# First batched stage of a four-layer kernel: normalising steps spread over evictions, transposes moved into the first block, zero matmuls while rows load

## The chip, the cores and the metric

The kernel runs on one core of a Trainium2 chip. Its engines run side by side, each with its own queue of instructions: TensorE (PE for matmuls, PEld for their weight loads), VectorE (DVE), ScalarE (ACT), GpSimd (POOL) and SyncE (SP), which only issues transfers. ACT and POOL issue transfers too, between their other instructions. The metric is the device time of one execution in microseconds (us); the time before is the median of five runs.

## The reference

Four layers, A B A B, each added to its input x of 2048 rows by 640. What matters here is layer A, whose first call is where the change lies:

```python
def _layernorm(x, axis=-1, eps=1e-05):
    m = jnp.mean(x, axis=axis, keepdims=True)
    v = jnp.var(x, axis=axis, keepdims=True)
    return (x - m) / jnp.sqrt(v + eps)
...
        for s in range(n_seg):
            xs = x[:, s * seg_len:(s + 1) * seg_len, :].copy()
            h = jnp.concatenate([mem, xs], axis=1)
            q = jnp.einsum('btd,dhe->bhte', h, Wq)
            k = jnp.einsum('btd,dhe->bhte', h, Wk)
            v = jnp.einsum('btd,dhe->bhte', h, Wv)
            ...
            o = jnp.einsum('bhte,hed->btd', o, Wo)
            mem = o[:, :M, :].copy()
            outs.append(o[:, M:, :])
...
    x = x + _A_ref(_layernorm(x, axis=-1), A_mem0, A_Wq, A_Wk, A_Wv, A_Wo, A_seg_len)
    x = x + _B_ref(_layernorm(x, axis=-1), B_wqkv, B_w_phi, B_wo)
```

There are 64 segments of 32 rows and a memory of 8 rows that passes from one segment to the next; 32 heads of 192 features. Layer B is an attention without a chain and is not touched.

## The kernel before

Layer A has two parts. `A_chain` walks through the 64 segments one after the other, since the memory of one is the output of the last. To shorten that chain, `A_pre`, the batched stage, computes ahead of it what does not depend on the memory: the last 8 rows of every segment ("tails") are projected to q, k and v for all segments at once and stored in HBM (`kqb_d`, `vb_d`). It also normalises all rows of x for the chain in the first layer (`xn_dram`), since no layer B before it has done so. The change is in this first call of `A_pre`, where `x_raw` is given.

The stage has eight blocks. A block is a half h of the segments (32 segments, 256 tail rows) and a round r of eight heads; the order is r=3 for h=0 and h=1, then r=2, r=1, r=0 (`steps`, L769). I number them 1 to 8. A block has

- K and Q: for each, six groups, each ten matmuls of 128x256 (L803) into one PSUM bank, then one eviction of 128x512 (L807);
- one store of the block's k and q to `kqb_d`, issued by ACT (L809, 1536 KB in pieces of 384 bytes);
- V: two row tiles k of four groups, each five matmuls of 128x384 (L820), an eviction (L822), and after each row tile four stores to `vb_d`, issued by POOL (L824).

There are eight PSUM banks, taken in turn, and 20 evictions in a block, by VectorE and ScalarE alternately (`Ev`, L77).

The weights of a round are 15 pieces of 384 KB, five each of Wk, Wq and Wv, issued by SP (`load_matrix`, L621) in the order of use. SP has nothing else in its queue, so it runs ahead of TensorE as far as its waits let it. Three pieces of each matrix go to slots that the next round of that kind reuses, so some pieces of r=0 wait for matmuls of r=3.

`norm_tasks` splits the normalising of one tile of 128 rows in four steps: a, the load; b, the statistics on VectorE and two casts on POOL (`ln_moments`, L216); c, two activations on ScalarE (`ln_deviation`); d, reciprocal, subtraction and scaling on VectorE (`ln_apply`) and what follows, a store to `xn_dram` or the use in the stage. `in_turn` lists these steps for many tiles so that the load of a tile stands ahead of the last three steps of the tile before it. The list `tasks` is worked off one step after each eviction (`evict`, L742): first the two tail tiles of h=1 (8 steps), then the 16 tiles of all rows (64 steps), from the first eviction of block 1. The two tail tiles of h=0 are done before block 1, in step (L762). Two buffers serve each tile kind.

`transpose_rows` (L705) turns a normalised tail tile into columns: five transposes on TensorE and one copy by VectorE or ScalarE. It is done at the start of block 1 for h=0 and at the start of block 2 for h=1 (L783).

`lay_out_wo` (L645) copies two rounds of Wo from HBM to HBM in another layout (`wo_rows`, 1920 KB each); ACT issues the two copies at the start of block 5. `build_A_consts` builds small constants at block 3. `early_wo` loads seven pieces of Wo on SP in block 8.

`A_chain` then starts with the Q projection of the first segment (L901), and `fill(FILL[li])` puts 122 weight loads of one column between it and the K projection in layer 0 (L987, L1052).

The stage's instructions stand in the order in which the program gives them on each engine (`manual_schedule`). Each transfer of SP and ACT is given one of eight completion semaphores, in turn over both engines, and waits for the transfer that had that semaphore before.

Of the kernel before, what the change touches and what calls it, by code (L numbers as in the profile page):

```python
# [8 lines left out]
P = 128  # L9
BF16 = mybir.dt.bfloat16  # L10
F32 = mybir.dt.float32
# [6 lines left out]
SLOTS = {"Q": 3, "K": 3, "V": 3}  # L18
LN_EPS = 1e-5

FILL = {0: 122, 2: 78}
SEG_FILL = 1

LATE = 64512
# [91 lines left out]
class Kernel:  # L116
# [96 lines left out]
        m = self.ln_moments(lp, xt)  # L213
        self.ln_apply(lp, xt, m, self.ln_deviation(lp, m), xn, centre, scale)

    def ln_moments(self, lp, xt):  # L216
        nc, Dm = self.nc, self.Dm
        half = Dm // 2
        stats = lp.tile([P, 2, 6], F32, name="ln_stats")
        for j in range(2):  # L220
            nc.vector.bn_stats(out=stats[:, j, :], in_=xt[:, j * half:(j + 1) * half])
        mv = lp.tile([P, 2], F32, name="ln_mv")
        nc.vector.bn_aggr(out=mv[:], in_=stats[:])
        mv16 = lp.tile([P, 2], BF16, name="ln_mv16")
        nc.gpsimd.tensor_copy(out=mv16[:], in_=mv[:])
        mvr = lp.tile([P, 2], F32, name="ln_mvr")
        nc.gpsimd.tensor_copy(out=mvr[:], in_=mv16[:])
        return mvr

    def ln_deviation(self, lp, mvr):  # L230
# [350 lines left out]
    def layer_A(self, xn_dram, at_dram, li, x_raw=None):  # L581
# [63 lines left out]
        def lay_out_wo():  # L645
            if li == 0:
                self.wo_rows = dram.tile([2, P, 7680], BF16, name="wo_rows")
                for i, r in enumerate((0, 3)):
                    nc.scalar.dma_start(out=self.wo_rows[i].rearrange("p (c m) -> p c m", m=640),
                                        in_=wov[:, 12 * r:12 * r + 12, :])  # L650

        def early_wo():
# [15 lines left out]
    def A_pre(self, xn_dram, li, load_matrix, piece, wo_mid, wo_end, lay_out_wo, early_wo, x_raw):  # L668
# [9 lines left out]
        NT = T // P  # L678
        sts = [wo_mid[:, 6144 * i:6144 * i + 192 * SH].rearrange("p (s f) -> p s f", f=192) for i in range(2)]
        vts = [wo_end[:, 1792 * i:1792 * i + 1792].rearrange("p (g f) -> p g f", f=448) for i in range(2)]  # L680
        with ExitStack() as es:
# [14 lines left out]
            def gather(dst, src, h, k, queues=None):  # L696
                xv = src.rearrange("(s t) d -> t s d", t=32)
                for t2 in range(TP):
                    e = queues[t2 % 2] if queues else nc.gpsimd if k % 2 else nc.scalar
                    e.dma_start(out=dst[SH * t2:SH * t2 + SH, :], in_=xv[24 + TP * k + t2, SH * h:SH * h + SH])  # L700
# [4 lines left out]
            def transpose_rows(xb, h, k):  # L705
                pt = ps_.tile([P, 1024], BF16, name="pt", tag="bank")
                for b in range(KC):
                    self.transp(out=pt[:, P * b:P * b + P], in_=xb.rearrange("p (q b) -> p b q", b=KC)[:, b, :],
                                identity=self.ident[:, :])
                ev.copy(out=columns(h)[:, :, P * k:P * k + P], in_=pt[:, 0:640].rearrange("p (b q) -> p b q", b=KC))  # L710

            def norm_tasks(load, done, tag="ln_xn"):

                v = {}

                def a():
                    v["x"] = lp.tile([P, self.Dm], BF16, name="ln_x")
                    load(v["x"])

                def b():  # L720
                    v["m"] = self.ln_moments(lp, v["x"])

                def c():
                    v["d"] = self.ln_deviation(lp, v["m"])

                def d():
                    xn = lp.tile([P, self.Dm], BF16, name=tag, tag=tag)
                    self.ln_apply(lp, v["x"], v["m"], v["d"], xn[:])
                    done(xn)

                return [a, b, c, d]

            def in_turn(lists):

                out = [lists[0][0]]
                for i, t in enumerate(lists):
                    if i + 1 < len(lists):
                        out.append(lists[i + 1][0])
                    out += t[1:]
                return out  # L740

            def evict(out, in_):  # L742
                ev.copy(out=out, in_=in_)
                if tasks:
                    tasks.pop(0)()

            normed = {}

            def tails(h):
                return in_turn([norm_tasks(lambda x, k=k: gather(x, x_raw, h, k),  # L750
                                           lambda xn, k=k: normed.__setitem__((h, k), xn), "ln_xt") for k in range(NT)])

            def all_rows():
                rows = [slice(P * b, P * b + P) for b in range(self.NB)]
                return in_turn([norm_tasks(lambda x, q=q: nc.gpsimd.dma_start(out=x[:], in_=x_raw[q, :]),
                                           lambda xn, q=q: nc.gpsimd.dma_start(out=xn_dram[q, :], in_=xn[:]))
                                for q in rows])

            for vt in vts:
                nc.vector.memset(vt, 0.0)  # L760
            if x_raw is not None:
                first = [norm_tasks(lambda x, k=k: gather(x, x_raw, 0, k, (nc.sync, nc.scalar)),  # L762
                                    lambda xn, k=k: normed.__setitem__((0, k), xn)) for k in range(NT)]
                for step in zip(*first):
                    for f in step:
                        f()
            turn = nv = 0
            if x_raw is not None:
                steps = [(h, ri, NR - 1 - ri) for ri in range(NR) for h in range(NH)]  # L769
# [1 line left out]
                steps = [(h, ri, ri if h == 0 and NH > 1 else NR - 1 - ri) for h in range(NH) for ri in range(NR)]  # L771
            seen = set()
            for h, ri, r in steps:
                if h not in seen:
                    seen.add(h)
                    xBT = columns(h)
                    for k in range(NT):
                        if x_raw is not None:
                            xb = normed[h, k]
                        else:  # L780
                            xb = xB[h][k % 2]
                            gather(xb, xn_dram, h, k)
                        transpose_rows(xb, h, k)  # L783
                xBT = columns(h)
                if (h, ri) == ((NH - 1, 0) if x_raw is None else (0, 2)):
                    lay_out_wo()
                st = sts[turn % 2]
                turn += 1
# [2 lines left out]
                if x_raw is not None and (h, ri) == (0, 0):  # L791
                    for h1 in range(1, NH):
                        tasks += tails(h1)
                    tasks += all_rows()
                for mi, m in enumerate("KQ"):
                    load_matrix(m, r)
# [17 lines left out]
                for k in range(NT):  # L814
                    vt = vts[nv % 2]
                    nv += 1
                    for g in range(4):
                        ps = ps_.tile([P, 512], F32, name="ps_pre", tag="bank")
                        for b in range(KC):
                            nc.tensor.matmul(ps[:, 0:384], lhsT=xBT[:, b, P * k:P * k + P],  # L820
                                             rhs=w[b][:, 384 * g:384 * g + 384], start=(b == 0), stop=(b == KC - 1))
                        evict(out=self.two_heads(vt[:, g, :]), in_=ps[:, 0:384].rearrange("p (e f) -> p e f", e=2))  # L822
                    for t2 in range(TP):
                        nc.gpsimd.dma_start(out=self.vb_d[SH * h:SH * h + SH, r, :, TP * k + t2, :],  # L824
                                            in_=vt[SH * t2:SH * t2 + SH, :, :].rearrange("p (g x) f -> p g (x f)", x=2))
# [367 lines left out]
```

## Time and profile before

| | us |
|---|---|
| median of five runs | 3762.22 |
| lowest and highest of the five | 3751.65, 3768.33 |
| the profiled execution, its own time | 3751.06 |
| span of the profiled execution | 3749.3 |
| first batched stage, from its first projection to the chain's first | 10.6 to 198.9 |

The profile page gives the span and the busy time of each engine. The other views are answers of the same trace: busy time by stretch; instructions in order of time, with the idle time of the engine before each and what ended it in square brackets; waits by line; and transfers with their median time from issue to landing. Line numbers are those of the kernel before. In the stage, transfers look like this over the first 200 us (queue 1 is SP's, queue 10 ACT's, queue 0 POOL's; then packets, MB and the share of 16 engines' time):

```profile
q1 hardware_dynamic: 10608, 26.06, 35.0%
q10 hardware_dynamic: 36183, 16.77, 30.4%
q0 software_dynamic: 4608, 12.11, 18.6%
```

### The profile page before, as it was taken

To read this page: it belongs to the slowest core of one execution; us is meant where nothing else is said; L and a number is where in the kernel's file an instruction comes from. 1 tells how busy PE (TensorE), PEld (TensorE's weight loads), DVE (VectorE), ACT (ScalarE), POOL (GpSimd) and SP (SyncE) were. 2 spreads that over 40 slices of the span, in tenths; PEclk is the share of its full clock that TensorE was granted. 3 is DMA by queue.
4 is the path that set the end of the run, shared out by engine and by line. 5 is a ranking of instruction groups with operands and counts; after the bars stand their busy time and mean duration, and the time that the engine had idled before them with its cause. 6 is when DMAs were issued, how large, how long until landed. Compare 5 with 4: busy or idle time off the path is not lost.

```text
span 3749.3 us, 169123 instructions
## 1 busy us (share of the span) xinstructions
PE 3539.8 (94%) x71064; PEld 2314.8 (62%) x71408; DVE 2364.7 (63%) x6290; ACT 2072.2 (55%) x5285; POOL 1658.2 (44%) x4363
## 2 busy tenths in 40 slices
PE   7989999999999999989899899999999999999898
PEld 5766666666666666655367566666666666665453
DVE  4456666666666666546633566666666666665565
ACT  2246666666666656546432556666666666665453
POOL 3345555555555545430342455555545555553300
PEclk9999999999999999999899999999999999999999
DMA  9788888788887878930377878878888888888200
GB/s 344 221 271 292 282 283 295 272 293 280 292 287 273 291 277 280 311 113 1 135 254 199 300 263 290 288 273 289 283 285 293 279 295 277 287 285 301 80 1 29
DMA packets 531381, 931.72 MB, mean 249 GB/s; under 512 B 141034, under 2 KB 298362, under 8 KB 530618
## 3 DMA queue, kind: packets, MB, share of 16 engines
q1 hardware_dynamic: 392794, 802.36, 60.3%
q0 software_dynamic: 68160, 88.78, 7.9%
q10 hardware_dynamic: 69664, 29.76, 3.0%
q8 instruction: 558, 9.14, 1.0%
q14 instruction: 205, 1.68, 0.1%
HBM read 852.43 MB, written 72.09 MB: 247 GB/s over the span
## 4 chain that ended last, share of the span: by engine, by line
PE 60%; DMA 10%; DVE 9%; issue 7%; ACT 6%; PEld 4%; POOL 3%; SPq 1%; POOLq 0%; ACTq 0%; DVEq 0%
PE ps_qk L901 19%; PE ps_w L977 8%; PE ps_v L901 8%; PE ps_o L951 5%; PE ps_s L943 4%; DMA arena<-wo_rows 4%; PEld L803 3%; DVE hT L857 3%; PE ps_s L1009 3%; PE ps_s L938 2%; PE ps_idle L984 2%; PE ps_qk L388 2%; ACT raw L911 2%; PE ps_pre L803 1%; DVE E L1016 1%
## 5 line engine op out<-in xcount | busy, mean ns | idle before, releaser
L901 PE MATMUL ps_qk<-arena,hT 128*32 128x384 bf16 x20480 | 1000.2, 328 | 23.7 <-DMA arena<-in_A_Wk_dram 8.9
L901 PEld LDWEIGHTS <-hT 128*32 128x32 bf16 x30720 | 737.8, 96 | 440.8 <-DVE hT L1119 29.4
L911 ACT ACTIVATE raw<-ps_qk 128x384 bf16<-128x384 f32 x1024 | 502.0, 490 | 395.0 <-PE ps_s L1009 247.6
L977 PE MATMUL ps_w<-arena,OT 128*32 128x160 bf16 x24576 | 538.5, 234 | 27.2 <-issue 18.6
L884 POOL DMA_DIRECT2D Vp<-vb x512 | 258.8, 505 | 674.9 <-PE ps_o L951 464.1
L901 PE MATMUL ps_v<-arena,hT 128*32 128x384 bf16 x10240 | 535.6, 329 | 0.0
L977 PEld LDWEIGHTS <-OT 128*32 128x32 bf16 x24576 | 433.9, 97 | 118.5 <-issue 41.3
L916 DVE STREAM_TRANSPOSE KT<-raw 128x384 bf16<-128x384 bf16 x512 | 296.1, 578 | 203.0 <-ACT raw L911 199.0
L919 DVE STREAM_TRANSPOSE QT<-raw 128x256 bf16<-128x256 bf16 x512 | 227.9, 445 | 238.6 <-ACT raw L911 197.2
L872 POOL DMA_DIRECT2D kqb<-kqb x512 | 286.0, 559 | 162.8 <-POOL KT L880 148.1
L932 DVE CAST Vp<-ps_v 64x384 bf16<-64x384 f32 x512 | 286.4, 559 | 89.9 <-ACT Vp L930 76.7
L970 POOL DMA_DIRECT2D otb<-otb x512 | 282.8, 552 | 111.3 <-DVE otb L966 91.5
L930 ACT ACTIVATE Vp<-ps_v 64x384 bf16<-64x384 f32 x512 | 246.1, 481 | 145.6 <-PE ps_v L901 109.7
L957 DVE CAST OT<-ps_o 128x192 bf16<-128x192 f32 x512 | 183.1, 358 | 221.0 <-PE ps_o L951 203.4
L1016 DVE TENSOR_TENSOR E<-E,ps_s 80x320 bf16<-80x320 bf16 x512 | 247.5, 483 | 73.2 <-ACT ps_s L1015 69.1
L995 ACT ACTIVATE E<-ps_s 80x320 bf16<-80x320 f32 x512 | 221.4, 432 | 127.4 <-PE ps_s L943 100.2
L951 PEld LDWEIGHTS <-Vp 80*128 80x128 bf16 x4096 | 183.1, 99 | 160.3 <-issue 126.1
L951 PE MATMUL ps_o<-E,Vp 80*128 80x80 bf16 x4096 | 234.2, 202 | 24.6 <-ACT Vp L930 4.5
L943 PE MATMUL ps_s<-QT,KT 128*80 128x80 bf16 (+1 forms) x3072 | 234.2, 214 | 21.2 <-DVE KT L916 10.9
L865 ACT ACTIVATE Vp<-ps_w 32x160 bf16<-32x160 f32 x512 | 150.3, 294 | 177.9 <-DVE wt L1118 149.6
L956 ACT ACTIVATE OT<-ps_o 128x192 bf16<-128x192 f32 x512 | 167.8, 328 | 143.5 <-PE ps_o L951 143.4
L943 PEld LDWEIGHTS <-KT 128*80 128x80 bf16 x3072 | 195.8, 119 | 69.8 <-issue 58.8
(148 smaller groups left out, 5456.1 us busy)
## 6 DMA issues: line engine op xcount, KB each, us to landing
arena<-wo_rows SPq DMA_DIRECT2D x792, 320.0 KB, 6.7
arena<-in_A_Wq_dram SPq DMA_DIRECT2D x427, 384.0 KB, 4.5
arena<-in_A_Wv_dram SPq DMA_DIRECT2D x427, 384.0 KB, 6.4
arena<-in_A_Wk_dram SPq DMA_DIRECT2D x768, 192.0 KB, 4.6
kqb<-arena ACTq DMA_DIRECT2D x16, 1536.0 KB, 12.0
kqb<-kqb POOLq DMA_DIRECT2D x512, 48.0 KB, 5.0
arena<-in_A_Wk_dram SPq DMA_DIRECT2D x43, 384.0 KB, 6.6
vb<-arena POOLq DMA_DIRECT2D x128, 112.0 KB, 5.4
```

The lines of the kernel that those rows point to most:

```text
L872: nc.gpsimd.dma_start(out=kqb[:], in_=self.kqb_d[s, :, r, :])
L884: nc.gpsimd.dma_start(out=Vs[n % 2][64:80, :], in_=self.vb_d[s, r].rearrange("g t f -> (g t) f"))
L901: nc.tensor.matmul(o[32 * g:32 * g + 32, 0:384], lhsT=hT[:, b, :], rhs=rhs, start=(i == 0), stop=(i == KC - 1), tile_position=(0, 32 * g), ...
L911: nc.scalar.activation(out=raw[:], in_=ps[:, 0:384], func=ACT.Copy)
L916: nc.vector.transpose(out=KT[:, :, 0:64], in_=raw[:, :].rearrange("p (c j) -> p c j", j=64))
L930: nc.scalar.activation(out=o, in_=i, func=ACT.Copy)
L932: nc.vector.tensor_copy(out=o, in_=i)
L943: nc.tensor.matmul(S[0:80, c0:c0 + 80 * (q1 - q0)], lhsT=KT[:, 3 * x + i, :], rhs=QT[:, x, q0:q1, :], start=False, stop=(x == 1 and i == 2 ...
L951: nc.tensor.matmul(O[x][:, 80 * i:80 * i + 80], lhsT=Vs[n % 2][0:80, 448 * x + k:448 * x + k + 128], rhs=E[0:80, 160 * x + 80 * e:160 * x ...
L970: nc.gpsimd.dma_start(out=self.otb_d[s, :, 96 * r:96 * r + 96], in_=otb[:, :, :].rearrange("p c t -> p (c t)"))
L977: nc.tensor.matmul(W[32 * g:32 * g + 32, 0:160], lhsT=OT[:, c, q:q + 32], rhs=w[:, 640 * i + 160 * g:640 * i + 160 * g + 160], start=(firs ...
L1016: nc.vector.tensor_tensor(out=E[0:80, 0:320], in0=E[0:80, 0:320], in1=rc, op=ALU.mult)
```

## The change

Seven things change, all but one of them in `A_pre` with `x_raw` given, that is in layer 0's stage.

1. `ln_moments` can take the engine of its two casts; the stage's tasks give VectorE instead of POOL. Layer B's calls keep POOL.
2. The list of tasks may hold empty steps, and an eviction that meets one does nothing more. The tails of h=1 get three empty steps after their two loads; the tiles of all rows get one after every two steps, so a tile takes six evictions instead of four.
3. The 16 tiles of all rows are queued from block 2 instead of block 1.
4. The transposes of h=1 are done inside block 1, after the first row tile of V.
5. `lay_out_wo` is called at the start of block 6 instead of block 5 and issued by SP instead of ACT, in the first layer.
6. Matmuls of the identity with a buffer of zeros, 128x512, into a bank of their own: 12 before the first transposes and 3 after each of the two sets of transposes of h=0. Nothing reads their result.
7. `FILL` for layer 0 goes from 122 to 86.

```diff
-FILL = {0: 122, 2: 78}
+FILL = {0: 86, 2: 78}
...
-    def ln_moments(self, lp, xt):
+    def ln_moments(self, lp, xt, cast=None):
...
-        nc.gpsimd.tensor_copy(out=mv16[:], in_=mv[:])
+        cast = cast or nc.gpsimd
+        cast.tensor_copy(out=mv16[:], in_=mv[:])
         mvr = lp.tile([P, 2], F32, name="ln_mvr")
-        nc.gpsimd.tensor_copy(out=mvr[:], in_=mv16[:])
+        cast.tensor_copy(out=mvr[:], in_=mv16[:])
...
                 for i, r in enumerate((0, 3)):
-                    nc.scalar.dma_start(out=self.wo_rows[i].rearrange("p (c m) -> p c m", m=640),
+                    (nc.sync if x_raw is not None else nc.scalar).dma_start(out=self.wo_rows[i].rearrange("p (c m) -> p c m", m=640),
                                         in_=wov[:, 12 * r:12 * r + 12, :])
...
-                    v["m"] = self.ln_moments(lp, v["x"])
+                    v["m"] = self.ln_moments(lp, v["x"], nc.vector)
...
                 ev.copy(out=out, in_=in_)
-                if tasks:
-                    tasks.pop(0)()
+                step = tasks.pop(0) if tasks else None
+                if step:
+                    step()
...
             def tails(h):
-                return in_turn([norm_tasks(lambda x, k=k: gather(x, x_raw, h, k),
-                                           lambda xn, k=k: normed.__setitem__((h, k), xn), "ln_xt") for k in range(NT)])
+                t = in_turn([norm_tasks(lambda x, k=k: gather(x, x_raw, h, k),
+                                        lambda xn, k=k: normed.__setitem__((h, k), xn), "ln_xt") for k in range(NT)])
+                return t[:NT] + [None] * 3 + t[NT:]
...
-                return in_turn([norm_tasks(lambda x, q=q: nc.gpsimd.dma_start(out=x[:], in_=x_raw[q, :]),
-                                           lambda xn, q=q: nc.gpsimd.dma_start(out=xn_dram[q, :], in_=xn[:]))
-                                for q in rows])
+                t = in_turn([norm_tasks(lambda x, q=q: nc.gpsimd.dma_start(out=x[:], in_=x_raw[q, :]),
+                                        lambda xn, q=q: nc.gpsimd.dma_start(out=xn_dram[q, :], in_=xn[:]))
+                             for q in rows])
+                return [f for i in range(0, len(t), 2) for f in (*t[i:i + 2], None)]
...
+                warm = ps_.tile([P, 512], F32, name="ps_warm", tag="bank")
+
+                def busy(n):
+                    for _ in range(n):
+                        nc.tensor.matmul(warm[:, :], lhsT=self.ident[:, :], rhs=vts[0].rearrange("p g f -> p (g f)")[:, 0:512],
+                                         start=True, stop=True, skip_group_check=True)
+
+                busy(12)
...
-                if h not in seen:
+                if h not in seen and (x_raw is None or h == 0):
...
                         transpose_rows(xb, h, k)
+                        if x_raw is not None:
+                            busy(3)
                 xBT = columns(h)
-                if (h, ri) == ((NH - 1, 0) if x_raw is None else (0, 2)):
+                if (h, ri) == ((NH - 1, 0) if x_raw is None else (NH - 1, 2)):
                     lay_out_wo()
...
                     for h1 in range(1, NH):
                         tasks += tails(h1)
+                if x_raw is not None and (h, ri) == (NH - 1, 0):
                     tasks += all_rows()
...
                         evict(out=self.two_heads(vt[:, g, :]), in_=ps[:, 0:384].rearrange("p (e f) -> p e f", e=2))
+                    if x_raw is not None and (h, ri, k) == (0, 0, 0):
+                        for h1 in range(1, NH):
+                            for k1 in range(NT):
+                                transpose_rows(normed[h1, k1], h1, k1)
```

## The prediction

> **What bounds the kernel now.** I read the page first, then busy time by stretch for the first stage, then the order of time on TensorE and on its suppliers, and last the DMA queues.
>
> ```profile
> span 3749.3 us, 169123 instructions
> PE 3539.8 (94%) x71064; PEld 2314.8 (62%) x71408; DVE 2364.7 (63%) x6290; ACT 2072.2 (55%) x5285; POOL 1658.2 (44%) x4363
> ```
>
> TensorE is busy 94% of the span, and the changed stage runs once, before layer 0: whatever it gains is some microseconds out of 3749. Cut at the starts of its eight blocks (block 1 is h=0, r=3; block 2 is h=1, r=3; then r=2, 1, 0 in pairs), with busy us of PE, PEld, DVE, ACT, POOL, the granted clock, the DMA share and GB/s:
>
> ```profile
> 10.60:40.90 30.30, 22.83 (x170) 17.65 (x170) 14.79 (x38) 8.18 (x21) 8.66 (x24) 0.92 1.05 379
> 40.90:63.20 22.30, 22.29 (x160) 16.95 (x160) 12.87 (x33) 5.08 (x12) 7.02 (x19) 0.87 0.94 339
> 63.20:92.40 29.20, 22.10 (x162) 16.49 (x160) 12.43 (x34) 6.50 (x18) 12.68 (x42) 0.94 0.98 357
> 92.40:116.30 23.90, 21.09 (x160) 15.59 (x160) 15.91 (x44) 7.93 (x23) 11.26 (x28) 1.00 0.70 206
> 116.30:140.10 23.80, 20.14 (x162) 15.66 (x161) 9.73 (x19) 6.15 (x13) 9.09 (x17) 1.00 1.04 316
> 140.10:159.70 19.60, 19.60 (x162) 15.66 (x161) 6.39 (x10) 5.54 (x10) 4.21 (x8) 1.00 0.67 197
> ```
>
> All blocks have the same 160 matmuls. Undisturbed, a block takes 19.60 us (block 6, and 7 and 8 alike). Blocks 1 to 5 take 10.7, 2.7, 9.6, 4.3 and 4.2 us more, 31.5 us in all: that is the most the change can win here. But the DMA share in blocks 1 to 3 is 0.94 to 1.05: the transfers are full just where TensorE waits.
>
> ```profile
> 10.63 15.77 PE L803 MATMUL ps_pre<-arena 128*128 128x256 bf16 x120 [0.79 <-ACT arena L89]
> 38.09 0.89 DVE L221 BATCH_NORM_STATS2 ln_stats<-ln_x 128x6 f32<-128x320 bf16 x2 [2.50 <-DMA ln_x<-in_A_x_dram]
> 40.91 15.98 PE L803 MATMUL ps_pre<-arena 128*128 128x256 bf16 x120 [7.46 <-ACT arena L89]
> 68.31 0.39 ACTq L809 DMA_DIRECT2D kqb<-arena  x1
> 69.22 0.87 ACT L89 ACTIVATE arena<-ps_pre 128x384 bf16<-128x384 f32 x2 [9.40 <-DMA arena<-in_A_Wv_dram]
> 116.45 4.30 ACTq L649 DMA_DIRECT2D wo_rows<-in_A_Wo_dram  x1
> 120.79 3.22 ACTq L649 DMA_DIRECT2D wo_rows<-in_A_Wo_dram  x1
> 159.68 13.26 PE L803 MATMUL ps_pre<-arena 128*128 128x256 bf16 x120
> ```
>
> Three losses show. The K and Q matmuls take 15.77 us after the start and 15.98 us after a 7.46 us gap, against 13.26 us in block 7. The gap itself stands because the transposed rows of h=1 are copied behind a normalising step of VectorE that waits 2.50 us for its x rows. And ScalarE stands 9.40 us before the second kqb store (68.31): a queued DMA blocks the evictions behind it. In the built order, each DMA of SP and ACT takes the next of eight completion semaphores and first waits for the DMA that last had it; this store waits for the fourth Wv piece of r=1. SP itself stood so at 30 us:
>
> ```profile
> SPq L625 <- DMA kqb<-arena: 14.7, 1, 14.7
> wo_rows<-in_A_Wo_dram ACTq DMA_DIRECT2D x2, 1920.0 KB, 18.2
> ```
>
> **The change, part by part.**
>
> *Zero matmuls.* 12 before the first transposes, 3 after each five. They need the identity and the memset of vts (done at 2.85 us); the first normed rows come at 7.55. A 128x512 product is twice a 128x256 one; the slow first groups take about 2.2 us for ten of those, so 12 cost at most 5.3 us and end near 8.2, some 0.4 us into the transposes, which are bounded by the second row tile anyway. The six later ones (below 0.25 us each at the rate of block 7) stand between row tiles. Gain: 15.77 - 13.26 = 2.5 us.
>
> [...]
>
> *Casts on VectorE.* A pair on POOL is 2 x 0.18 us plus two handovers: from the end of L223 to the start of L234 it takes 0.53 us at the first tile. On VectorE, near the 0.06 to 0.16 us of its small operations, the pair is about 0.2. At the start that is worth 0.2 us net (the second tile's casts now stand before the first tile's apply). Elsewhere the 18 pairs, under 4 us of VectorE, lie in its idle time (block 4, its fullest, has 15.91 of 23.90).
>
> *Transposes of h=1 inside block 1.* The ten transposes (0.72 us) stay; the 7.46 us gap and the slow run behind it (15.98 - 13.26 = 2.7) go: 10.2 us. The condition is that both tail tiles are ready after the first four V groups, near 27 us. Their four ACT x loads now wait, by their semaphores, up to the third Wq piece (issued 6.66, landing after 7.3, so 14 us), which puts the rows at 14 + 5.9 = 20, the eviction behind them at 21 and both tiles at 27. Just in time; at the worst 1 us late.
>
> *Spreading.* A row tile takes six evictions in place of four; from load to statistics there are now eight evictions (8 us) in place of four, for loads that land after 5.7 to 6.3 us. All 16 tiles end in block 6, which has VectorE at 6.39 of 19.60. What the statistics and POOL cost blocks 3 to 5 goes, 1.2 + 2.7 + 3.0 us of idle TensorE in blocks 3 and 4 and some part of block 5.
>
> *The copy of Wo rows from ACT to SP.* It frees ACT of 4.30 + 3.22 = 7.5 us (3 us of idle TensorE in block 5). But SP does not wait for block 6: in the built order the two copies stand on SP right behind the Wv pieces of r=1 and ahead of all r=0 pieces. SP prefetches, so they start near 57 us instead of 116, in the fullest stretch. And the third kqb store on ACT, in block 3, now waits by its semaphore for the last Wk piece of r=0, behind both copies. Behind it stand the evictions on ACT, and behind them TensorE with its eight banks.
>
> [...]
>
> *FILL 122 to 86.* 122 take 1.96 us, so 36 are 0.58 us. Soon after, TensorE waits for Wo pieces (a 0.70 us wait at 212, more up to 226), which are issued by the end of the stage, not by the fill: 0. Bounds: 0.6 gained; 2.5 lost if the clock falls as at the start.
>
> **The sum.** Without new waits: start 10.4, block 1 with its transposes to 30.8, block 2 to 50.4.
>
> New wait 1: the second kqb store (due at 45) waits for the fourth Wq piece of r=1. Before, a piece five places later landed at 68.3; a piece of 0.39 MB then took 1.1 us (SP's queue moved 3.49 MB from 60 to 70 us): 62.8. SP leads by about 4 us (two Wv pieces of r=2 no longer stand behind the first kqb store, 2.2 us, and I allow 1.8 for the slack that this store leaves behind): 58.8. The bank that TensorE wants in the second group of block 3 (51.5) is free 0.9 us later (issue and eviction), at 59.7: 8.2 us, and 2.5 us of slow clock. Block 3 ends 18.5 us of work later, at 80.7.
>
> New wait 2: the last Wk piece of r=0 was issued at 64.6 and landed 9.6 later: 74.2, less the lead, 70.2. The copies come on top. Their own time is the ACT queue's share from 116.4 to 139.2 (83.2% of 22.8 us, 5.80 MB) less 1.87 MB of kqb at 260 GB/s: 11.8 us. From issue to landing the pair took 22.8 us. So the piece lands between 82.0 and 93.0; I take the middle, 87.5, since kqb and POOL traffic share the engines as they did then. The bank is free 0.9 us later, 88.4; TensorE came for it at 81.8. Block 4 ends 18.5 + 2.5 later, 109.4; blocks 5 to 8 take 78.4: 187.8, where it was 198.9. So 11.1 us are won, with some of the fill 11.5: the profiled execution (3751.06, span 3749.3) becomes 3739.5, and the median, 11.2 us above that execution, 3750.7. The bounds of the copies alone give 3745 to 3757.
>
> **Rivals.**
> 1. *The copies do not hold up Wk.* If the piece lands before 81, only wait 1 is left (10.7 us): the stage ends at 168.0 + 10.7 = 178.7, 20 us are won, 3742. Without wait 1 as well it is 31 us, 3731. For it: the queue's own share was 89.6% at 60 to 70 us. Against: 3.93 MB must pass the same engines.
> 2. *DMA sets the stage's end.* The piece lands at 97 to 100: stage end 197 to 200, time 3761 to 3764. For it: shares of 0.94 to 1.05 up to 92 us, and 3.93 MB moved into that stretch.
> 3. *The copies starve the weights: slower.* Each copy took 18.2 us. If on SP they run one after the other, with two kqb stores and POOL between, Wk lands at 70.2 + 36.4 + 6 = 113 and the stage ends at 213: 14 us lost, 3776. It decides from a landing at 99. Against it: the two overlapped on ACT.
>
> **How the numbers follow.** Forecast 0.50, rival 1 0.30, rival 2 0.13, rival 3 0.07. A measurement of this kernel tells about 0.3%, 11.3 us, from no change. All of rival 1 and a little over half of the forecast are faster by more (0.57); the rest of the forecast and rival 2 are within it (0.37); slower 0.06, nearly all of rival 3. The range, 3733 to 3762, takes in the bounds of the copies, most of rival 1 and the lower edge of rival 2.
>
> **What would show it.** Right: no 7.46 us gap; first K and Q matmuls in about 13.3 us; blocks 5 to 8 at 19.6 us each; ACT waiting in blocks 2 and 3 for its second and third kqb store, with Wq and Wk as releasers, and TensorE idle some 8 us near 52 and 7 us near 82. Wrong: block 4 starting without such a wait, wo_rows landing under 12 us after its issue, or the transposes of h=1 waiting for VectorE.

## The result and the profile after

| | before | after |
|---|---|---|
| median | 3760.94 us (60 runs) | 3752.13 us (35 runs) |
| lowest and highest | 3746.34, 3771.45 | 3742.99, 3764.26 |
| span of the profiled execution | 3749.3 us | 3744.2 us |
| first batched stage ends (the chain's first projection) | 198.97 us | 192.67 us |
| idle TensorE in the stage behind ScalarE's evictions | 12.5 us | 15.1 us |

The ratio is 0.9977, 95% interval [0.9971, 0.9983]: 8.8 us less, under the 0.3% that was set as the bound of "faster". The forecast was 3750.7. In the profiled executions the stage gives 6.3 us of it, and eight segments into the chain the gain is 7.0.

The first lines of the profile page, span and busy time of each engine, for the kernel after:

```profile
span 3744.2 us, 169085 instructions
PE 3548.7 (95%) x71082; PEld 2317.4 (62%) x71390; DVE 2370.1 (63%) x6330; ACT 2074.7 (55%) x5285; POOL 1662.9 (44%) x4323
```

Busy time by stretch, cut at 10.50 and at the starts of blocks 2 to 6 (block 1 begins at 9.49 with four matmuls and two short waits; start:end, length, then busy us of PE, PEld, DVE, ACT, POOL, granted clock, DMA share, GB/s):

```profile
10.50:30.98 20.48, 19.80 (x167) 15.78 (x168) 10.75 (x27) 6.09 (x14) 2.08 (x4) 1.00 1.03 377
30.98:50.58 19.60, 19.60 (x162) 15.66 (x161) 10.46 (x30) 4.63 (x11) 5.50 (x11) 1.00 0.97 320
50.58:79.82 29.24, 22.62 (x161) 17.13 (x160) 11.04 (x31) 6.18 (x16) 10.09 (x31) 0.82 1.04 382
79.82:114.18 34.36, 23.16 (x162) 16.83 (x160) 14.54 (x43) 7.76 (x21) 8.10 (x15) 0.85 0.98 346
114.18:133.78 19.60, 19.60 (x162) 15.65 (x160) 14.35 (x42) 7.06 (x18) 10.44 (x20) 1.00 0.85 246
```

Blocks 1 and 2 are mended: 21.49 us from the first matmul at 9.49 (20.48 from 10.50) and 19.60 us, where 30.30 and 22.30 stood. Block 5 too. Blocks 3 and 4 are as long as before or longer: 29.24 (29.20 before) and 34.36 (23.90 before). The gains of the first two blocks are largely given back there. TensorE in order of time says to whom:

```profile
11.18 12.90 PE L818 MATMUL ps_pre<-arena 128*128 128x256 bf16 x116 [0.71 <-DMA arena<-in_A_Wk_dram]
...
27.17 0.72 PE L166 MATMUL pt<-ident,ln_xt 128*128 128x128 bf16 x10
...
61.73 11.76 PE L818 MATMUL ps_pre<-arena 128*128 128x256 bf16 x80 [6.62 <-ACT arena L89]
...
92.02 11.39 PE L818 MATMUL ps_pre<-arena 128*128 128x256 bf16 x90 [8.46 <-ACT arena L89]
...
107.63 6.71 PE L835 MATMUL ps_pre<-arena 128*128 128x384 bf16 x30 [2.60 <-DVE arena L87]
...
192.67 1.00 PE L920 MATMUL ps_qk<-arena,hT 128*32 128x384 bf16 x20
```

The transposes of h=1 (27.17) run inside block 1 without a gap. TensorE then stands 6.62 us in block 3 and 8.46 us in block 4 for a bank that ScalarE (L89) has not emptied, and 2.60 us in block 4 for one of VectorE. ScalarE itself:

```profile
60.60 0.39 ACTq L824 DMA_DIRECT2D kqb<-arena  x1
61.19 0.87 ACT L89 ACTIVATE arena<-ps_pre 128x384 bf16<-128x384 f32 x2 [13.53 <-DMA arena<-in_A_Wq_dram]
...
90.91 0.37 ACTq L824 DMA_DIRECT2D kqb<-arena  x1
91.48 0.49 ACT L89 ACTIVATE arena<-ps_pre 128x384 bf16<-128x384 f32 x1 [17.36 <-DMA arena<-in_A_Wk_dram]
```

Before each of the two kqb stores (L824) ScalarE is idle, 13.53 and 17.36 us, released by the landing of a weight piece, Wq and Wk: the two new waits of the prediction. SyncE's queue shows what holds that Wk piece:

```profile
59.51 7.94 SPq L650 DMA_DIRECT2D wo_rows<-in_A_Wo_dram  x2
67.50 10.43 SPq L626 DMA_DIRECT2D arena<-in_A_Wk_dram  x2
78.05 1.53 SPq L620 DMA_DIRECT2D arena<-in_A_Wk_dram  x3
```

The two copies of Wo rows stand ahead of the Wk pieces of r=0: they begin at 59.51, and the last three of these pieces are issued from 78.05 on, 18.5 us later. The 2.60 us of VectorE in block 4 go back to x rows:

```profile
105.44 0.89 DVE L221 BATCH_NORM_STATS2 ln_stats<-ln_x 128x6 f32<-128x320 bf16 x2 [7.65 <-DMA ln_x<-in_A_x_dram]
```

and the load of these rows stands on GpSimd behind stores of v that wait for ScalarE (17.12 us idle before the first line):

```profile
93.05 2.15 POOL L843 DMA_DIRECT2D vb<-arena  x4 [17.12 <-ACT arena L89]
95.78 0.57 POOL L758 DMA_DIRECT2D ln_x<-in_A_x_dram  x1
```

So the 2.60 us go back to a load that stands behind the block's stores of v and whose rows are there 9.7 us after its issue. It looks like a second bill for the wait that ended at 90.91, with everything behind it late. The experiments do not bear that out: a wait of 2.5 to 3.7 us stands at this place in x_wo_act, x_wo_late and x_k23_pool too, where TensorE waits for no held store in block 4.

### The profile page after: what moved, and what is told of

Read it like the earlier page. It is cut to its first block, busy times and chain, and to the rows that moved or that the text cites. A ratio compares the mean times of both kernels' runs of the same rounds, so it can differ in the third digit from the quotient of the medians.

```text
span 3744.2 us, 169085 instructions
## 1 busy us (share of the span) xinstructions
PE 3548.7 (95%) x71082; PEld 2317.4 (62%) x71390; DVE 2370.1 (63%) x6330; ACT 2074.7 (55%) x5285; POOL 1662.9 (44%) x4323
## 5 line engine op out<-in xcount | busy, mean ns | idle before, releaser
L996 PE MATMUL ps_w<-arena,OT 128*32 128x160 bf16 x24576 | 539.9, 234 | 22.2 <-issue 12.9
```

The lines of the kernel that those rows point to most:

```text
L996: nc.tensor.matmul(W[32 * g:32 * g + 32, 0:160], lhsT=OT[:, c, q:q + 32], rhs=w[:, 640 * i + 160 * g:640 * i + 160 * g + 160], start=(firs ...
```

## The experiments

Each kernel but x_no_warm, which ran once, ran several times in turn with the kernel before on the same chip. Beside these runs the kernel before took 3773 to 3777 us, 12 to 16 more than beside the result, so only ratios and points in the trace are compared. Two points are read from each profile: where the stage ends (the chain's first projection), and, to see whether something is given back soon after, the start of the 32nd product of `ps_s<-E,ones_blk`, eight segments into the chain (a segment has four of them).

| kernel | stage ends | 32nd product | ratio to before, 95% interval |
|---|---|---|---|
| before | 198.97 | 379.30 | 1 |
| after (result) | 192.67 | 372.29 | 0.9977 [0.9971, 0.9983] |
| r_after, the same again | 193.03 | 374.37 | 0.9973 [0.996, 0.9986] |
| x_wo_act | 186.64 | 370.16 | 0.995 [0.9934, 0.9966] |
| x_wo_late | 183.53 | 363.33 | 0.9956 [0.9942, 0.997] |
| x_kqb_pool | 197.13 | 366.95 | 0.9949 [0.9935, 0.9964] |
| x_kqb_pool_wo_late | 198.39 | 367.56 | 0.9945 [0.9928, 0.9963] |
| x_k2_pool | 184.95 | 368.07 | 0.9948 [0.9931, 0.9965] |
| x_k23_pool | 177.86 | 359.03 | 0.9904 [0.9884, 0.9925] |
| x_no_spread | 208.35 | 387.28 | 1.0014 [1.0003, 1.0024] |
| x_warm_tiny | 189.66 | 371.49 | 0.9957 [0.9933, 0.9981] |
| x_no_warm, x_no_warm_b | 186.84, 188.49 | 375.80 (the second) | 1.028 [1.0247, 1.0312] (the second) |
| b_fill86 | 198.77 | 388.12 | 1.0307 [1.028, 1.0334] |

The intervals are some 0.3% wide, about 11 us; a few microseconds of the stage are read from the traces, not from them. One program profiled twice ended its stage at 192.67 and 193.03 us (the changed kernel), another at 186.84 and 188.49 (without zero matmuls), so differences under 2 us in the first column say nothing.

**r_after: the changed kernel beside the experiments.**

> The changed kernel itself, beside the others on one chip. Its stage should end at 192.7 us within 1 us again, with the same two waits of ScalarE (13.5 and 17.4 us), and its time should be 0.9977 of the kernel before within 0.0015. If the ratio here is 0.995, as for the kernels run before it on this chip, the chip decides the difference and not the place of the copies.

The stage ended at 193.03 and the ratio was 0.9973: the result stands here too.

**x_wo_act: the copies of Wo rows back on ScalarE.**

```diff
-                    (nc.sync if x_raw is not None else nc.scalar).dma_start(out=self.wo_rows[i]...
+                    nc.scalar.dma_start(out=self.wo_rows[i]...
-                if (h, ri) == ((NH - 1, 0) if x_raw is None else (NH - 1, 2)):
+                if (h, ri) == ((NH - 1, 0) if x_raw is None else (0, 2)):
                     lay_out_wo()
```

> The two copies of Wo rows go back to ScalarE at block 5; all else is the changed kernel. Theory T (ScalarE is held by kqb stores that wait for weight pieces, and the copies ahead of the r=0 pieces make the second of these waits long): the 8.46 us idle of TensorE in block 4 goes with its 2.5 us of slow clock and most of the 2.60 us wait for x rows, the wait in block 3 stays at 6 to 9 us, block 5 pays about 3 us for ScalarE's issue of the copies: the stage ends at 180 to 187 us (192.7 with the copies on SyncE), 6 to 12 us faster than the changed kernel. Rival D (the transfers themselves set the end of the stage, whatever their order): stage end 191 to 195, the same time as the changed kernel within 2 us.

The stage ended at 186.64 us, 6.0 before the changed kernel. TensorE in order of time:

```profile
64.85 10.68 PE L818 MATMUL ps_pre<-arena 128*128 128x256 bf16 x80 [9.24 <-ACT arena L89]
...
84.72 12.17 PE L818 MATMUL ps_pre<-arena 128*128 128x256 bf16 x110 [1.59 <-DVE arena L87]
...
101.59 6.71 PE L835 MATMUL ps_pre<-arena 128*128 128x384 bf16 x30 [3.08 <-DVE arena L87]
```

The 8.46 us in block 4 became 1.59. The wait in block 3 grew from 6.62 to 9.24, since the second store now has its turn with a Wv piece, which lands later than the Wq piece. The wait for x rows, 3.08 us here, did not go with the held store as expected, and block 5 did not pay the 3 us that were expected (it took 19.61 us): moving these copies off ScalarE won nothing here and cost 6 us. Rival D, that the transfers as such set the end of the stage, falls: the same bytes pass, and the stage ends outside its range.

**x_wo_late: the copies on SyncE, behind the last Wv pieces of r=0.**

```diff
-                if (h, ri) == ((NH - 1, 0) if x_raw is None else (NH - 1, 2)):
+                if x_raw is None and (h, ri) == (NH - 1, 0):
                     lay_out_wo()
...
                 load_matrix("V", r)
+                if x_raw is not None and (h, ri) == (0, NR - 1):
+                    lay_out_wo()
```

> The two copies stay on SyncE but stand behind the last Wv pieces of r=0. T: as with the copies on ScalarE, without the 3 us in block 5, but the third kqb store now waits for the last Wq piece of r=0, which lands later than the third: some 0 to 6 us in block 4. Stage end 178 to 187, 6 to 14 us faster than the changed kernel. D: stage end 191 to 195, no difference beyond 2 us.

The stage ended at 183.53, 9.1 before the changed kernel, with TensorE idle 9.73 us in block 3, and 1.22 and 2.52 in block 4. Not the engine that issues the copies matters but their place among the weight pieces.

**x_kqb_pool and x_kqb_pool_wo_late: all kqb stores of layer 0 on GpSimd**, the second with the copies late.

```diff
-                nc.scalar.dma_start(out=self.kqb_d[SH * h:SH * h + SH, :, r, :]...
+                (nc.gpsimd if x_raw is not None else nc.scalar).dma_start(out=self.kqb_d[SH * h:SH * h + SH, :, r, :]...
```

> The kqb stores of layer 0 are issued by GpSimd, the copies stay ahead of the r=0 pieces. T: no eviction of ScalarE stands behind a store, so both waits (6.62 and 8.46 us) and their slow clock (5 us) go, though the last Wk piece of r=0 still lands near 90 us, since nothing needs it before block 7: stage end 168 to 176, 17 to 25 us faster than the changed kernel. If GpSimd's issue of a 4096-piece store is slow, its x loads come late and VectorE's waits for x rows grow: then the stage ends somewhere between 176 and 195, with DVE waiting for ln_x. D: stage end 191 to 195 with TensorE waiting for weight pieces in place of evictions.

> The kqb stores of layer 0 on GpSimd, and the two copies on SyncE behind the last Wv pieces of r=0. T: with ScalarE free of the stores the place of the copies matters little: stage end 168 to 175, within 3 us of the kernel that has only the stores moved. D: 191 to 195.

Half of T, the theory of the held stores, came true: no eviction of ScalarE waits for a piece any more, and block 5 starts at 105.26 and 100.75 us, where the changed kernel has 114.18. But the chain started at 197.13 and 198.39, outside the range. TensorE with all stores on GpSimd (x_kqb_pool):

```profile
50.58 8.55 PE L835 MATMUL ps_pre<-arena 128*128 128x384 bf16 x40 [6.68 <-DVE arena L87]
...
197.13 1.79 PE L920 MATMUL ps_qk<-arena,hT 128*32 128x384 bf16 x20 [13.30 <-DVE hT L876]
```

and GpSimd there:

```profile
42.39 0.54 POOL L843 DMA_DIRECT2D vb<-arena  x1 [9.16 <-DMA kqb<-arena]
43.13 1.15 POOL L758 DMA_DIRECT2D ln_x<-in_A_x_dram  x2 [0.20 <-DMA arena<-in_A_Wv_dram]
```

The coupling moved with the stores: GpSimd's transfers take turns with completion semaphores too, so a store of v waits 9.16 us for a kqb store to land, and the x loads, and at the end of the stage the chain's first loads, stand behind it. Of the 13.30 us at the start of the chain about ten come back at once, since the Wo, Wq and Wk pieces that the chain waits for in the other kernels have landed by then: at the 32nd product this kernel is 12.4 us ahead of the kernel before.

**x_k2_pool and x_k23_pool: only the stores that had waited.** The copies late as in x_wo_late, and the second, or the second and third, store on GpSimd. The line is that of x_k23_pool; x_k2_pool has (1, 0) alone.

```diff
-                nc.scalar.dma_start(out=self.kqb_d[SH * h:SH * h + SH, :, r, :]...
+                (nc.gpsimd if x_raw is not None and (h, ri) in ((1, 0), (0, 1)) else nc.scalar).dma_start(out=self.kqb_d[SH * h:SH * h + SH, :, r, :]...
```

> The copies of Wo rows on SyncE behind the last Wv pieces of r=0, and the second kqb store alone issued by GpSimd; the other seven stay on ScalarE. T: TensorE's 9.73 us in block 3 (seen with the copies late) goes with its slow clock; x rows come later, since GpSimd's next x load waits for that store, which costs TensorE 3 to 6 us in blocks 3 and 4; the last stores are not on GpSimd, so the 13 us wait at the start of the chain is gone: stage end 172 to 180, 13 to 20 us before the changed kernel. Rival: the wait only moves to VectorE's x rows in full, stage end 183 or more.

> The copies behind the last Wv pieces of r=0, the second and third kqb stores issued by GpSimd, the others by ScalarE. T: no eviction stands behind a store in blocks 2 to 4: the 8.36 us that TensorE lost in block 4 with only the second store moved goes, with most of its slow clock; GpSimd's waits for two stores cost 3 to 6 us more of waits for x rows. Stage end 176 to 181. Rival: x rows take all of it, 184 or more.

With one store moved the stage ended at 184.95, on the rival's side, but not for the rival's reason: TensorE idled 8.4 us behind ScalarE again, now at the third store, which had its turn with the last Wq piece. With both moved no wait on ScalarE is left in the stage (waits of TensorE in x_k23_pool from 0 to 178 us: total, times, longest):

```profile
PE ps_pre L837 <- DVE arena L87: 4.8, 3, 3.7
PE ps_pre L818 <- DVE arena L87: 3.0, 2, 2.5
PE ps_warm L775 <- DVE arena L764: 2.0, 1, 2.0
PE pt L166 <- DVE ln_xn L245: 1.5, 1, 1.5
PE ps_pre L818 <- DMA arena<-in_A_Wk_dram: 0.9, 2, 0.7
```

and blocks 3 and 4 take 22.75 and 24.12 us at a granted clock of 1.00:

```profile
51.59:74.34 22.75, 19.92 (x162) 15.64 (x160) 10.43 (x31) 5.74 (x15) 10.42 (x32) 1.00 1.02 385
74.34:98.46 24.12, 19.92 (x162) 15.64 (x160) 13.63 (x40) 5.54 (x15) 8.85 (x15) 1.00 1.03 401
```

The stage ended at 177.86, inside T's range, 14.8 us before the changed kernel. Its DMA shares of 1.02 and 1.03 are like the 1.04 and 0.98 of the changed kernel, so a full DMA was not what held that one. This version is the fastest of all: 3738.4 us median, 0.9904 of the kernel before.

**x_no_spread: the steps of a row tile without the empty ones.**

```diff
-                return [f for i in range(0, len(t), 2) for f in (*t[i:i + 2], None)]
+                return t
```

> A row tile's steps follow one another without the empty ones: from load to statistics four evictions in place of eight, sixteen tiles done in two thirds of the evictions. If the spreading is worth what the prediction put on it, TensorE loses up to some 7 us more in blocks 2 to 4 to VectorE's waits for x rows: stage end 195 to 200. If ScalarE's two waits cover it: stage end 192 to 194.

The stage ended at 208.35, 15.7 later than in the changed kernel, beyond both expectations. Its waits of TensorE up to 209 us:

```profile
PE ps_pre L818 <- ACT arena L89: 14.8, 2, 9.7
PE ps_pre L818 <- DVE arena L87: 9.0, 6, 2.7
PE ps_pre L835 <- DVE arena L87: 5.3, 2, 3.8
```

ScalarE's two waits add up to as much as before (14.8 against 15.1 us), and 14.3 us behind VectorE come on top, where the changed kernel has 2.6. But the run does not price the spreading alone, since the third store has its turn with another piece here, first TensorE, then ScalarE:

```profile
102.66 12.78 PE L818 MATMUL ps_pre<-arena 128*128 128x256 bf16 x90 [9.73 <-ACT arena L89]
...
101.55 0.37 ACTq L824 DMA_DIRECT2D kqb<-arena  x1
102.12 0.87 ACT L89 ACTIVATE arena<-ps_pre 128x384 bf16<-128x384 f32 x2 [16.99 <-DMA arena<-in_A_Wv_dram]
```

It waits for a Wv piece and goes out at 101.55, in the changed kernel for a Wk piece and at 90.91. TensorE behind it goes on at 102.66, not at 92.02: that is 10.6 of the 15.7 us, and 5.0 come after it. TensorE had come to this point at 92.9, so the waits behind VectorE alone would have put it 0.9 us behind the changed kernel here; by these rows the spreading is worth about 0.9 + 5.0 = 5.9 us, an estimate.

**x_no_warm and x_warm_tiny: without zero matmuls, and with 18 of 32 columns in place of 512.**

```diff
-                busy(12)
...
-                        if x_raw is not None:
-                            busy(3)
```

> The 18 zero matmuls are left out (they add nothing to the output). By the prediction's step the first K and Q matmuls take 15.8 us after their first wait where they now take 12.90 with 0.9 us of waits for Wk pieces before: stage end 2.0 to 2.6 us later, 194.7 to 195.3. Rival: the Wk pieces set the first block anyway, under 1 us.

It took 3858.8 us, 100 more than the changed kernel, and yet its stage ended 5.8 us earlier. Neither side was expected. Two runs took this apart, the small matmuls first:

```diff
-  nc.tensor.matmul(warm[:, :], lhsT=..., rhs=vts[0]...[:, 0:512], ...
+  nc.tensor.matmul(warm[:, 0:32], lhsT=..., rhs=vts[0]...[:, 0:32], ...
```

> The 18 zero matmuls are kept, 32 columns wide in place of 512: the same number of instructions on TensorE, next to no work. The built program gives the DMAs the same completion semaphores as without any zero matmuls. If that numbering made ScalarE's waits shorter there (2.74 and 4.22 us of idle TensorE in blocks 3 and 4 where the changed kernel has 6.62 and 8.46), the stage ends again at 185 to 188 us, with the slow clock of about 2.7 us in the first block. If the program's length on TensorE was behind the slow chain without zero matmuls (3858.8 us), this one, which has the changed kernel's length, takes 3750 to 3765.

> Again the changed kernel without zero matmuls, now timed. If the 100 us that it lost after the stage were one bad execution, its time is 3750 to 3760 and the stage ends at 186 to 188 again. If they belong to the program: 3840 to 3870, with TensorE waiting for issue at the output projections of the chain.

x_no_warm_b took 3881.37 us (4 runs): the loss belongs to the program. x_warm_tiny did without it (0.9957), and its stage ended at 189.66, 3.0 before the changed kernel although its first matmuls are slow. In order of time, first TensorE, then ScalarE:

```profile
11.13 14.82 PE L818 MATMUL ps_pre<-arena 128*128 128x256 bf16 x116 [0.30 <-DMA arena<-in_A_Wk_dram]
...
60.34 0.38 ACTq L824 DMA_DIRECT2D kqb<-arena  x1
60.93 0.87 ACT L89 ACTIVATE arena<-ps_pre 128x384 bf16<-128x384 f32 x2 [11.94 <-DMA arena<-in_A_Wq_dram]
...
87.89 0.37 ACTq L824 DMA_DIRECT2D kqb<-arena  x1
88.46 0.49 ACT L89 ACTIVATE arena<-ps_pre 128x384 bf16<-128x384 f32 x1 [14.32 <-DMA arena<-in_A_Wk_dram]
```

116 matmuls take 14.82 us where the changed kernel needs 12.90. Cut into microseconds, the trace has 6 or 7 of them in each from 12 to 15 us and 12 from 16 us on, where the changed kernel has 11 or 12 from 12 us on. The rate is halved there, as in the kernel before, which has 12 of these matmuls from 12 to 14 us; the granted clock of that stretch is 1.00 in the kernel before and in the changed one, so it is not shown that the clock halves it. But ScalarE waits 11.94 and 14.32 us in place of 13.53 and 17.36. The second store goes out nearly when it did, at 60.34 in place of 60.60: ScalarE only comes to it later, as the first block is slower. The third goes out at 87.89 in place of 90.91, and these 3.0 us are those of the stage. In the built program the order of the two queues has moved a little without the long zero matmuls, and the two stores take turns with earlier weight pieces, the third Wq piece in place of the fourth and the second Wk piece in place of the fifth. Without any zero matmuls it is the first Wk piece (x_no_warm), so the order was not quite the same as the expectation says.

**b_fill86: the kernel before with FILL 86.**

```diff
-FILL = {0: 122, 2: 78}
+FILL = {0: 86, 2: 78}
```

> The kernel before with FILL 86 in place of 122: 36 instructions fewer on TensorE ahead of the chain's later segments, as without the 18 zero matmuls and their 18 weight loads. Theory L (the chain's speed hangs on how many instructions TensorE has had before it; the kernels before and after both have 142,894, the slow one 142,858): 1.02 to 1.03 of the kernel before, with some 100 us and more of TensorE waiting for issue at the output projections. The prediction's step (FILL costs nothing, at most 0.6 us won or 2.5 lost): the same time within 0.1%. Rival to L: zero matmuls matter for the clock or the order of the chain and not by their number, then this kernel keeps its speed too.

3893.37 us, 1.0307 of the kernel before, with a stage that ends at 198.77. TensorE in the chain, b_fill86:

```profile
433.62 0.58 PE L977 MATMUL ps_w<-arena,OT 128*32 128x160 bf16 x23
435.81 0.66 PE L977 MATMUL ps_w<-arena,OT 128*32 128x160 bf16 x25 [1.60 <-issue]
```

and the kernel before at the like place:

```profile
252.31 0.30 PE L977 MATMUL ps_w<-arena,OT 128*32 128x160 bf16 x5
253.22 0.94 PE L977 MATMUL ps_w<-arena,OT 128*32 128x160 bf16 x43 [0.60 <-issue]
```

"issue" is idle time for which the profile shows no wait. In the chain TensorE stands so nearly always at one place, inside the third of a segment's four output projections of 48 matmuls each: after the fifth matmul in the kernel before, after the 23rd in b_fill86. That is 18 matmuls with 18 weight loads later, just the 36 instructions that were taken away ahead of it. So the place is fixed in the stream of TensorE's instructions, counted from its start. It is the same in every segment because a segment, some 22 us, is 1,024 instructions of TensorE, in the built program and in the trace. Of the 128 segments of both A layers, 31 have the wait in the kernel before and 113 in b_fill86. The sums over the whole execution, first b_fill86 (us, times, longest):

```profile
PE ps_w L977 <- issue: 127.9, 113, 2.7
```

then the kernel without zero matmuls (x_no_warm_b), which stands after the 23rd too:

```profile
PE ps_w L993 <- issue: 127.5, 110, 2.5
```

The kernel before has 18.6 us in 31 such waits, the changed one 12.9 in 31, x_warm_tiny 16.1 in 33. So theory L holds: before and after both have 142,894 instructions on TensorE, and the two slow ones 142,858. The 18 zero matmuls with their 18 weight loads make up for the 36 weight loads taken from the fill. The smaller fill without them costs over 100 us (b_fill86, x_no_warm_b), with them nothing; the zero matmuls with the old fill were not run.

The profiles show a queue for instructions, with 558 packets in the kernels before and after and in x_no_warm_b (packets, MB, share of 16 engines' time). In the first 200 us of the kernel before ten of them pass, beside 1,320 matmuls and 1,329 weight loads. Over the whole execution there are 142,894 / 558 = 256 instructions of TensorE to a packet; if the queue serves TensorE alone, an estimate from these counts, a segment of 1,024 takes four:

```profile
q8 instruction: 558, 9.14, 1.0%
```

After the 23rd matmul a wait is 127.9 / 113 = 1.1 us as a mean, after the fifth 18.6 / 31 = 0.6 us. The times of these packets go with the waits: all 144 waits of the kernel before and b_fill86 end 1.20 to 1.67 us after such a packet has landed, though the packets come some 6 us apart. That these packets are what TensorE waits for is the author's reading; it is not shown, since no run changed them alone. Why it would be one packet in four, and more often after the 23rd matmul, stays open. That the place in the stream decides is shown.

## Why the prediction was right, and where it was not

- *The first two blocks.* Block 1 was to end at 30.8 and block 2 at 50.4; they ended at 30.98 and 50.58. The tail tiles of h=1 were in time. The first matmul came at 9.49, not at 10.4, and two short waits for Wk pieces (0.21 and 0.71 us) took that back.
- *New wait 1.* Bank free at 59.7 and block 3 ending at 80.7 were forecast; 61.7 and 79.82 came. TensorE got four groups of ten matmuls into block 3, not one, before it lacked a bank, so it idled 6.62 us in place of 8.2.
- *New wait 2.* The last Wk piece was put at 87.5, between 82.0 and 93.0; the store that waited for it was issued at 90.91. TensorE's idle time was 8.46 us, 6.6 forecast. The mechanism was right, copies on SyncE ahead of the pieces that ScalarE's store waits for, and x_wo_act and x_wo_late show it by removing it.
- *What the sum missed in block 4.* It took 14.8 us over an undisturbed block, 9.1 forecast. Of the 5.7 us between, 2.60 are a wait for x rows, which the prediction held for gone with the spreading; 1.9 are the longer wait for the store; 1.1 are slow matmuls (TensorE busy 23.16 us against 19.60, that is 3.6 more where 2.5 were put, at a granted clock of 0.85). Less the 0.9 us that block 3 ended early, this is the stage's whole error of 4.9 us (192.67, not 187.8).
- *FILL at nothing: this step failed.* Its cost was looked for in the time of the weight loads (0.58 us) and in Wo pieces that come late anyway; bounds of 0.6 won and 2.5 lost. By itself it costs 3.1%, some 117 us. The forecast was saved only because the zero matmuls put the 36 instructions back, which it did not see: that was luck.
- *Zero matmuls at -2.5 us: right for the first matmuls, wrong for the sum.* The 12 ahead of the transposes took 4.82 us; at most 5.3 were forecast. Without any zero matmuls the first K and Q matmuls take 15.88 us (x_no_warm_b, 120 of them), 2.6 over the undisturbed 13.26. That the clock is low at the start is not shown: the granted clock is 1.00 from 12 to 14 us with 12 matmuls (before) and with 21 (after). But TensorE only waits longer in block 3 for it: it comes there 1.9 us earlier than in x_warm_tiny, where they do next to nothing (50.58 and 52.45), and stands 6.62 us in place of 1.35 + 2.98. And x_warm_tiny ends its stage 3.0 us earlier, since its third store has its turn with an earlier piece: by the order of the queues that they bring about in this program, the zero matmuls cost more than they win.
- *The spreading* was priced at 1.2 + 2.7 + 3.0 = 6.9 us of idle TensorE in blocks 3 and 4, and some part of block 5. Without it the stage ends 15.7 us later, but 10.6 of these are lost by the end of a longer wait for the third store, which has its turn with another piece there; the rows point to about 5.9 us, an estimate.
- *The copy of Wo rows.* The 7.5 us freed on ScalarE were counted as 3 us of TensorE in block 5. With the copies back on ScalarE their issue takes it 0.65 + 2.19 = 2.8 us and block 5 takes 19.61 us: nothing of it was on the path any more. Not even the time of issue was won by another issuer, the place in the new queue cost, and the move is a pure loss of 6.0 us.
- *Rivals.* Rival 1 (the copies do not hold up Wk) and rival 3 (they starve the weights) did not come; rival 2's range of 197 to 200 lies above the 192.67 measured, and that the bytes do not set the end is shown by x_k23_pool.
- *The total.* The forecast of 3750.7 us lies closer to the 3752.13 measured than its parts do, which is in part luck: 11.5 us were to be won and 8.8 were, and half of the difference is made up by a kernel before whose median is 1.3 us lower in sixty runs than in the five that were known. The bounds of the copies, 5.5 us either way, give 3745 to 3756, not 3757.

Left open: of the time that the best version wins over the kernel before, about 36 us (0.0096 of 3773; the interval allows 28 to 44), the stage accounts for 21.1 and the first eight segments confirm 20.3; where the rest is won was not found. Most experiments show such an excess, and no profile of the kernel before was taken beside them. The casts on VectorE and the place of the transposes were not tried alone.

## What to carry to other kernels

Where two engines' transfers take turns over eight completion semaphores, as in this program, a transfer waits for whatever had its semaphore before, and everything behind it on the issuing engine waits too, 13.53 and 17.36 us on ScalarE here: when an edit moves or adds a transfer, list for each store in the stretch whose landing it now waits for, and put only those stores elsewhere that wait for something late. A wait need not vanish when it is moved to another engine; look at what is queued there, as the x loads and the chain's first loads behind GpSimd's stores in x_kqb_pool, where a store of v waited 9.16 us. What is won ahead of a wait whose end is set by something else is lost in the wait, as the 1.9 us of the zero matmuls in block 3. Where a loop is unrolled in a fixed number of instructions, count TensorE's instructions ahead of it before adding or removing any, even idle ones: 36 weight loads fewer made this kernel 3.1% slower (b_fill86).

## What the runs showed of the hardware that was not expected

- TensorE stands, in some segments, at a place that is fixed in its instruction stream, once in 1,024 instructions; after the fifth of 48 matmuls it costs 0.6 us as a mean (18.6 in 31 waits), after the 23rd 1.1 us and in three to four times as many segments (127.9 in 113). Each of these waits ends 1.20 to 1.67 us after a packet of the instruction queue has landed.
- A kqb store of 1536 KB takes ScalarE 0.37 to 0.43 us to issue when nothing holds it and GpSimd 1.7 to 1.8 us; in x_k23_pool the two stores issued by GpSimd landed after 13.4 us (median), the one by ScalarE after 24.7, later in the stage, so it is not shown that the engine makes the difference.
